# Seven block products for the gate of the last two token groups and the value of groups three and four, with the output projection's products chained in PSUM

## The chip, the cores and the metric

The kernel runs on one core of one Trainium2 chip. The metric is the device time of one execution in microseconds (us); the median of the runs is taken. Matmuls are float16 with float32 sums in PSUM, inputs and output are float32. TensorE is PE (weight loads: PEld), VectorE DVE, ScalarE ACT, GpSimd POOL, SyncE SP.

## The reference

Attention for 4 batches of 8 heads, 768 positions of width 64, then a gated feed-forward layer on all 3072 tokens (512 to 1536 to 512). Heads 0, 2 and 6 see all earlier positions, the others the first 4 and the last 64.

```python
scores = scale * q @ k.T                  # masked: causal, or causal and (first 4 or last 64)
a = softmax(scores)
x = (a @ v), heads side by side           # 3072 x 512
g = x @ w_gate                            # 512 -> 1536
val = x @ w_val
out = (g * sigmoid(g) * val) @ w_out      # 1536 -> 512
```

## The kernel before, in words

**Attention.** The 3072 tokens are 24 tiles of 128. For each tile TensorE makes blocks of scores (L568) in PSUM, ScalarE takes the exponential of up to 1024 columns at a time into a tile `e` (L580), VectorE or GpSimd multiplies the blocks that need it by a mask (L588, 1024 or 640 columns), TensorE multiplies with the values (L598), VectorE divides by the sums (L605, L606), and TensorE turns the result so that tokens lie along columns, tile `xt`. Queries, keys, values and weights come as float32 into staging tiles `raw` by DMA from SP's queue and are cast to float16 on any of the three element-wise engines (L207 on ACT, L209 on POOL, L213 on DVE as a reduction over one element).

**Feed-forward.** Six groups of 512 tokens (g = 0 to 5), twelve hidden slices of 128 (j). A gate or a value of one slice is four matmuls of 512 columns (L760); in the first slices of group 0 it is made in halves. In groups 0 to 3 ScalarE takes a tanh of the gate (L766) and VectorE makes the silu from it (L773); in groups 4 and 5 ScalarE takes silu itself (L782), in place in PSUM. VectorE multiplies silu and value into the hidden tile `h_sb` (L787).

**Seven products.** A product of two matrices cut into 2 x 2 blocks can be made of seven block products instead of eight, with sums of blocks before (left and right) and sums of products after. The output projection is made so in all six groups: sums of blocks of the hidden tile (`hsum`, L844, tiles `h_sb` and `hs_sb`) and of the output weights (`wsum`, L413, tile `wt_sb`), seven products of twelve matmuls of 256 columns (`seventh`, L873), and eight sums or copies of the products into `out_sb` (`gathered`, L899 to L911; a copy is L207 or L209). The value of groups 4 and 5 is made so too: sums of the value weights (`msum`, L1066), of the tokens (`xsum`, L1096), three times seven products of four matmuls of 256 columns per group (`w_product`, L1116; products 6, 7 and 4 are summed onto product 1 in its PSUM room, 3 onto 5), and copies and sums into cells in `raw` tiles (`w_copy`, L207 and L209; `w_add`, L1137). The hidden tile is then made at L1166 from silu in PSUM and the cells.

**PSUM** is one tile `banks` of eight banks. Gate, value, products, scores and attention results each take a bank from it.

**Order.** All work is a list of tasks, one per step and group. Three tables written into the file set everything: ORDER is the order in which the tasks' instructions are issued, WAYS the engine of each task that has a choice (ACT, DVE, POOL or SP), SLOTS the buffer that each task takes from a ring. `Plan.order` reads them and a loop at the end runs the tasks. Each engine has its queue and works it off in that order; a semaphore holds an instruction back until its inputs are made and its buffer is free. ORDER also holds warm-up matmuls on an identity matrix (L322) at the start.

Of the kernel before, what the change touches and what calls it, by code (L numbers as in the profile page):

```python
# [28 lines left out]
    "CN5SCMCR5x5yCOC06O615zCXC17O5eCGC2C36A655kBq0f6v6xBjCYBr725jC47PCIBl718eCHBtBs6Q6U6RBk6VCeBu0eCA"
    "6WCf0c6SCg6B626CCJChCB6TCCBvCiCSBw6DBb70C5Bx6G6eCTByC66yBpC77F6X6Z0d7GBzC86YCZ7HC96a757CCa6n6FCb"  # L30
    "Bm6o817Q6b6c76CqCDCs826dDf7DBnCc77BoDr7E7WCEE1Ds7XDtDcE2Cd7RDu89CrDdE4E3CtDe7U7879DD7A6MCo6gDvDE"
    "7LDgDmDF7BCuE5DGDnCp7VDXCvDHDoDI88DYDZ6z7Y6k7bDJ7S6lDKDS7ZDa6m7j7IDb7JDTDp8f7K7cE6Dq6fDU6p7m6hE7"
    "E8E96i7dDN80EA6jDL6q86Dw7M7a7N6r6sDx7nD06tDODy6u7p7eD1Cw7x7fDM7q8387DP8A7T8D7sCx8BD2Cz7gD3DV7t7o"
    "DhDW7h7rDiD47i7k8EDjEa8ND6D585Cy8G8YD88H7uD7DQ8ZEc7vDR8I8W7y7wEtDk8J8C8X8F8T8QDl8K8L8g8UDzEb8hEu"
    "D98O7l8RE0Ee7z8i8jFNEf8M84Ev8VEgDC8kF0EhDAElEi8SDBEmFf8lEj8PF1EwF8Fg8aEEExEG8bEk8cFiEdF98dEpFjEn"
    "EBF2EqEoFAEyF4FBEDEzECErF3FCEsFQFkFFFRF5FlFGEFFDGQFhEHFmEJFOFPF6GMEKFEFTFSEIF7FWFJGNFXGXFUFYENGR"
    "GOFVFKGSGPFZEOGTFLFHFaGbFMGUFnFrEMFIFoGVHCFpGYFqGfGWGZFbGgFcFsGcGhFdELEPGaGiHDH9EQGdHAGjGeFuGkFe"
    "GqHEGuFtERGvFvGmESHRFwGwHSETGnGoGlEVEWGrEZFzEUHFHBHUHTHGG0GpHXGxHHHIEXHYG2HVH1GsHWHaG1GtHLHZHbHJ"
    "HcGyEYH5H2FxHMGzHOH6G3G5HPH3HdHKG4H0H7G8H4G9H8HeFyHNG7GFG6HQHfHgHlGAGBHhHiHnGDGCGGGIHmGEHjGJGHGK"
    "HzHoHkGLHqHpI3HrHtHvHsHuI4I5HxHwI0I6HyI2I9I7I1ICI8IAIBIDIE"  # L40
# [15 lines left out]
SLOTS = (
    "00142310557834203A728948194837A04374026281030677514571900124020502261616103140412010360010742002"
    "236101614442404106323200562004446120020050132024120000236504202044214005012342616560130400140430"
    "240426501210360012203622541636200122642522142261412021420360620216124236133056022234060254441411"
    "780000311241110210450107121300620173022210651247116100100135016400676677625122602120071100001361"  # L60
    "104112402751261023401751233542301411151104107112101006005400571246015012341114102541540201005110"
    "511141044005511251001120110140204023502454467623349741A203756436562602000262530310914A5433224054"
    "7117736756524224510144"
# [57 lines left out]
def kernel(  # L121
# [13 lines left out]
    nc = tc.nc  # L135
# [87 lines left out]
    SEVENS = 6  # L223
# [530 lines left out]
    hs, gs, sg, sl, vs, o_open, o_sbs = {}, {}, {}, {}, {}, {}, {}  # L754
# [37 lines left out]
    def pieces(g, tt):  # L792


        if g < NG - 1:
            return [("o", 0, DM)]
        if tt < SIZES[g] - 1:
            return [("o", 0, DM)]
        return [("gv", 0, DM - 128), ("gv", DM - 128, DM)]

    def outproj(g, tt, x, js):
        ring, lo, hi = pieces(g, tt)[x]
        if js.start == 0:
            o_open[g, tt, x] = buf(ring, [128, DM], FP, "o_ps")[:, lo:hi]
        for j in range(js.start, js.stop):
            nc.tensor.matmul(
                o_open[g, tt, x], hs[g, j][:, tt * 128:(tt + 1) * 128], wo_sb[:, j, lo:hi],
                start=(j == 0), stop=(j == NJ - 1))

    T_oe, T_st = {}, {}  # L810

    def oevac(g, tt, x):
        if x == 0:
            o_sbs[g, tt] = out_sb[:, tt // 2, tt % 2]
        ring, lo, hi = pieces(g, tt)[x]
        copy(T_oe[g, tt, x], o_sbs[g, tt][:, lo:hi], o_open.pop((g, tt, x)))

    def store(g, tt, x):

        b, i = TILES[FIRST[g] + tt]  # L820
        r0 = b * S + i * 128
        ring, lo, hi = pieces(g, tt)[x]
        eng = nc.scalar if T_st[g, tt, x].way == "ACT" else nc.sync
        eng.dma_start(out=out[r0:r0 + 128, lo:hi], in_=o_sbs[g, tt][:, lo:hi])
# [23 lines left out]
    ONTO = {2: 1, 3: 5}  # L848
    PARTS = [(0, 0, HM), (1, 0, HM)]
    APART = (1, 5)  # L850

    def seventh(g, p, part):
# [9 lines left out]
        on = ONTO.get(p) if g == NG - 1 else None  # L862
# [8 lines left out]
        for x, lo, hi in todo:  # L871
            for j in range(NK):
# [7 lines left out]
    CELLS = {"r1": (1, (1, 0), None), "c11": (2, (0, 0), (1, 0)), "r6": (6, (0, 1), (1, 0)),  # L880
             "r67": (7, (1, 1), (0, 1)), "c21": (4, (1, 0), (1, 1)), "r56": (5, (0, 1), (0, 1)),
             "c22": (5, (1, 1), (1, 1)), "c12": (3, (0, 1), (0, 1))}

# [5 lines left out]
    def gathered(g, name, part):  # L889
        p, to, other = CELLS[name]  # L890
# [22 lines left out]
    def store_cell(g, name, part):  # L913
        x, y = CELLS[name][1]
# [22 lines left out]
    def last_sevens(g, lower, upper, wo, free, old, T_h, product, sums, gather, finish):  # L937
        p1 = product(1, lower + wo, ["big"])
        r1 = gather("r1", [p1], takes=["raw"])
        sums(1, lambda part: [y for j in range(3 * part, 3 * part + 3)  # L940
                              for y in T_h[j] + T_h[j + NK]] + old)
        sums(3, lambda part: [T_hs[g, 1][part]])
        sums(2, lambda part: [T_hs[g, 3][part], p1])
        sums(4, lambda part: [T_hs[g, 2][part]], apart=True)
# [4 lines left out]
        p4 = product(4, upper + T_ws[4], ["o"])  # L949
# [9 lines left out]
        for part in range(2):  # L959
            p2 = product(2, upper + wo + [r1], (), part)  # L960
# [273 lines left out]
    for g in range(NG):  # L1234
# [8 lines left out]
        for j in range(NJ):  # L1243
            parts = [(0, 256), (256, 512)] if g == 0 and j < HALVES else [(0, w)]
            for c in parts:
                below = ("c11", "c21") if j < NK else ("c12", "c22")
                head = "r1" if j < NK else "u2"
                if g in SILU:
                    late = [y for y in P.tasks if y.name.startswith(f"ex{len(TILES) - 1}.")]
                    last_of_g = T_wc["g", g, j % NK // 2, head] if g in WINO["g"] else None  # L1250
                    if last_of_g is None:
# [7 lines left out]
                        if g not in WINO["v"]:  # L1259
                            P.uses(a, "gv", s1)  # L1260
# [118 lines left out]
```

## Time and profile before

| | before |
|---|---|
| median of 3 runs | 237.0 us (236.6 to 237.05) |
| span of the profiled execution | 234.7 us |
| granted TensorE clock | 1.00 |
| busy PE | 229.1 us (98%) |
| busy DVE | 191.6 us (82%) |
| busy ACT | 157.4 us (67%) |
| busy POOL | 137.4 us (59%) |
| DMA, mean | 40.76 MB, 174 GB/s |

The profile is of one execution. A share is busy time over the span. In a slice or a stretch of the span a digit is the busy share in tenths. A row of a timeline has the start and the duration in us, then engine, source line, operation, output and inputs with partitions x columns and type, and in brackets how long the engine was idle before, and what ended that. Two instructions that follow each other on VectorE or GpSimd overlap by up to 0.1 us in the rows.

### The profile page before, as it was taken

To read this page: it belongs to the slowest core of one execution; us is meant where nothing else is said; L and a number is where in the kernel's file an instruction comes from. 1 tells how busy PE (TensorE), PEld (TensorE's weight loads), DVE (VectorE), ACT (ScalarE), POOL (GpSimd) and SP (SyncE) were. 2 spreads that over 40 slices of the span, in tenths; PEclk is the share of its full clock that TensorE was granted. 3 is DMA by queue.
4 is the path that set the end of the run, shared out by engine and by line. 5 is a ranking of instruction groups with operands and counts; after the bars stand their busy time and mean duration, and the time that the engine had idled before them with its cause. 6 is when DMAs were issued, how large, how long until landed. Compare 5 with 4: busy or idle time off the path is not lost.

```text
span 234.7 us, 5842 instructions
## 1 busy us (share of the span) xinstructions
PE 229.1 (98%) x2283; PEld 153.1 (65%) x2283; DVE 191.6 (82%) x347; ACT 157.4 (67%) x254; POOL 137.4 (59%) x151
## 2 busy tenths in 40 slices
PE   7899999999999999999999999999999999999994
PEld 2677865655457778655564556777776767667883
DVE  1889989989999999999879974889968666667864
ACT  3599999679988769856786289767764464463000
POOL 7485499874696300488840887273096960845850
PEclk9999999999999999999999999999999999999999
DMA  6999999999999999998994721700910000220045
GB/s 178 351 343 367 327 336 368 344 341 312 272 258 223 215 246 195 256 169 193 224 235 124 105 45 28 65 3 7 225 39 6 0 0 3 89 89 3 0 183 179
DMA packets 67196, 40.76 MB, mean 174 GB/s; under 512 B 25184, under 2 KB 61024, under 8 KB 67168
## 3 DMA queue, kind: packets, MB, share of 16 engines
q1 hardware_dynamic: 65104, 37.37, 65.0%
q10 hardware_dynamic: 2064, 3.02, 3.7%
q8 instruction: 18, 0.29, 0.5%
q14 instruction: 10, 0.08, 0.1%
HBM read 28.31 MB, written 6.29 MB: 147 GB/s over the span
## 4 chain that ended last, share of the span: by engine, by line
PE 90%; ACT 3%; DMA 2%; SPq 2%; DVE 1%; issue 1%; ACTq 0%
PE banks L760 45%; PE banks L873 24%; PE banks L1116 8%; PE banks L568 6%; PE banks L598 6%; DMA raw<-in_k_dram 2%; ACT e L580 2%; SPq L350 1%; PE banks L474 1%; PE banks L622 1%; DVE xb L606 1%; ACT kT L207 0%; SPq L355 0%; DVE kT L209 0%; ACT hq L207 0%
## 5 line engine op out<-in xcount | busy, mean ns | idle before, releaser
L760 PE MATMUL banks<-xt,wg_sb 128*128 128x512 f16 (+1 forms) x304 | 71.1, 368 | 0.1
L580 ACT ACTIVATE e<-banks 128x1024 f16<-128x1024 f32 (+2 forms) x68 | 59.4, 910 | 10.7 <-PE banks L568 8.5
L760 PE MATMUL banks<-xt,wv_sb 128*128 128x512 f16 (+1 forms) x208 | 48.1, 363 | 0.0
L760 PEld LDWEIGHTS <-wg_sb 128*128 128x128 f16 x304 | 28.6, 98 | 26.1 <-issue 0.5
L873 PEld LDWEIGHTS <-h_sb 128*128 128x128 f16 x420 | 40.2, 98 | 6.9
L766 ACT ACTIVATE sig<-banks 128x512 f32<-128x512 f32 (+1 forms) x52 | 28.8, 567 | 14.6 <-PE banks L760 10.6
L773 DVE SCALAR_TENSOR_TENSOR sil<-sig,banks 128x512 f32<-128x512 f32 (+1 forms) x52 | 32.7, 640 | 4.9 <-ACT sig L766 4.0
L844 POOL TENSOR_TENSOR h_sb<-h_sb 128x768 f16<-128x768 f16 x14 | 22.9, 1639 | 22.7 <-DVE hs_sb L844 17.2
L787 DVE SCALAR_TENSOR_TENSOR h_sb<-sil,banks 128x512 f16<-128x512 f32 (+1 forms) x52 | 32.8, 639 | 2.9 <-PE banks L760 2.6
L588 POOL TENSOR_TENSOR e<-e,m 128x640 f16<-128x640 f16 (+1 forms) x16 | 26.6, 1669 | 7.3 <-ACT e L580 5.6
L911 DVE TENSOR_TENSOR out_sb<-banks,out_sb 128x512 f32<-128x512 f32 x37 | 25.1, 684 | 7.0 <-PE banks L873 6.8
L760 PEld LDWEIGHTS <-wv_sb 128*128 128x128 f16 x208 | 19.1, 98 | 17.4 <-POOL wv_sb L209 0.2
L782 ACT ACTIVATE banks<-banks 128x512 f32<-128x512 f32 x24 | 13.7, 587 | 19.2 <-PE banks L760 19.2
L873 PE MATMUL banks<-wt_sb,h_sb 128*128 128x256 f16 x216 | 26.1, 273 | 0.0
L873 PE MATMUL banks<-wo_sb,h_sb 128*128 128x256 f16 x204 | 25.1, 273 | 0.0
L207 ACT COPY raw<-banks 128x512 f32<-128x512 f32 x26 | 14.8, 593 | 12.0 <-PE banks L1116 6.5
L568 PEld LDWEIGHTS <-kT 64*128 64x128 f16 x472 | 14.5, 94 | 9.4 <-issue 8.9
L209 POOL CAST hq<-raw 128x1024 f16<-128x1024 f32 (+1 forms) x9 | 8.1, 895 | 20.6 <-DMA raw<-in_k_dram 18.8
L568 PE MATMUL banks<-qT,kT 64*128 64x128 f16 x472 | 19.9, 218 | 0.1
L598 PEld LDWEIGHTS <-e 128*128 128x128 f16 x472 | 17.3, 97 | 3.6 <-POOL e L588 0.3
L1166 DVE SCALAR_TENSOR_TENSOR h_sb<-banks,raw 128x512 f16<-128x512 f32 x24 | 15.9, 684 | 4.4 <-ACT banks L782 3.6
L598 PE MATMUL banks<-vt,e 128*128 128x65 f16 x472 | 18.6, 193 | 0.0
(86 smaller groups left out, 320.8 us busy)
## 6 DMA issues: line engine op xcount, KB each, us to landing
raw<-in_v_dram SPq DMA_DIRECT2D x12, 512.0 KB, 6.7
raw<-in_q_dram SPq DMA_DIRECT2D x8, 512.0 KB, 5.7
raw<-in_k_dram SPq DMA_DIRECT2D x8, 512.0 KB, 5.0
raw<-in_moe_w_gate_dram SPq DMA_DIRECT2D x6, 512.0 KB, 8.3
raw<-in_moe_w_val_dram SPq DMA_DIRECT2D x6, 512.0 KB, 8.3
raw<-in_moe_w_out_dram SPq DMA_DIRECT2D x6, 512.0 KB, 8.4
out_dram<-out_sb SPq DMA_DIRECT2D x6, 512.0 KB, 4.0
raw<-in_q_dram SPq DMA_DIRECT2D x8, 256.0 KB, 6.7
```

Source lines behind the costliest of these rows:

```text
L568: nc.tensor.matmul(sc[:, c:c + n, :], weights, moving, start=first, stop=last)
L580: nc.scalar.activation(out=to, in_=src, func=AF.Exp, scale=scale)
L588: ENG[task().way].tensor_tensor(out=ev, in0=ev, in1=mm, op=ALU.mult)
L598: nc.tensor.matmul(avs[t][:, odd, n * 66:n * 66 + 65], ee, vv, start=(m == 0), stop=(m == len(bl) - 1))
L760: nc.tensor.matmul(ps, wsb[:, kk, j * 128:(j + 1) * 128], xt[:, kk, c[0]:c[1]], start=(kk == 0), stop=(kk == 3))
L766: nc.scalar.activation(out=sg[g, j, c], in_=gs[g, j, c], func=AF.Tanh, scale=0.5)
L773: nc.vector.scalar_tensor_tensor(out=sl[g, j, c], in0=sg.pop((g, j, c)), scalar=1.0, op0=ALU.add, in1=gs.pop((g, j, c)), op1=ALU.mult)
L787: nc.vector.scalar_tensor_tensor(out=hs[g, j][:, c[0]:c[1]], in0=sl.pop((g, j, c)), scalar=1.0 if g in SILU else 0.5, op0=ALU.mult, in1=vs ...
L844: ENG[T_hs[g, x][part].way].tensor_tensor(out=to, in0=a, in1=b, op=op)
L873: nc.tensor.matmul(rooms[g, p][:, x, lo:hi], left[:, j, 128 * x:128 * x + 128], right[:, j, lo:hi], start=(on is None and (j == 0 if apart ...
L911: nc.vector.tensor_tensor(out=cell(*to), in0=room, in1=plus, op=ALU.add)
L1116: nc.tensor.matmul(w_rooms[on][:, m], right, left[:, kk], start=(begins and m == 0 and kk == 0), stop=(kk == 1), skip_group_check=True)
```

## The change

- The value of groups 2 and 3, and the gate of groups 4 and 5, are made of seven block products each, like the value of groups 4 and 5 before. So 24 gate tasks and 24 value tasks of four 512-column matmuls go, and 84 block products of four 256-column matmuls come, with their copies and sums, and with sums of the gate weights in the tiles `kT` and `vt` of the attention.
- Where gate and value are both made so (groups 4 and 5), silu is taken cell by cell (`w_silu`, L1134 of the changed kernel) and the hidden tile is made cell by cell: on DVE (L1154) or, new, on POOL (L1151), for 2 slices x 256 tokens.
- In the output projection of groups 0 to 4, products 6, 7 and 4 are summed onto product 1 in its PSUM room, and 3 onto 5 (`CHAIN`). Of the sums, r6, r67 and c21 become copies (u2, u3, c21), and r56 goes. The last group keeps its old form (`CELLS_END`).
- ORDER, WAYS and SLOTS are new. Four warm-up matmuls are fewer.
- Functions that were not in use are removed.

```diff
-    "06000307090A01081U1V0D041cxl1W1X0C021d1f0B20211g1e280g1i2229231h2B2A1j0m1r2C0h1Y1p1s2D1a0F1Z2N1q"
+    "06070A08090D0C0B1U1V031c0200041W011X051d1b1a2022231Y1Z211e0h0n0E0g0m0F0Gy11f1g1h1i1j1p1r2X1q1k1l"
...
-    WINO = {"v": (4, 5), "g": ()}
+    WINO = {"v": (2, 3, 4, 5), "g": (4, 5)}
...
     ONTO = {2: 1, 3: 5}
+    CHAIN = {6: 1, 7: 1, 4: 1, 3: 5}
...
-        on = ONTO.get(p) if g == NG - 1 else None
+        on = (ONTO if g == NG - 1 else CHAIN).get(p)
...
-    CELLS = {"r1": (1, (1, 0), None), "c11": (2, (0, 0), (1, 0)), "r6": (6, (0, 1), (1, 0)),
-             "r67": (7, (1, 1), (0, 1)), "c21": (4, (1, 0), (1, 1)), "r56": (5, (0, 1), (0, 1)),
-             "c22": (5, (1, 1), (1, 1)), "c12": (3, (0, 1), (0, 1))}
+    CELLS = {"r1": (1, (1, 0), None), "c11": (2, (0, 0), (1, 0)), "u2": (6, (0, 1), None),
+             "u3": (7, (1, 1), None), "c21": (4, (1, 0), None),
+             "c22": (5, (1, 1), (1, 1)), "c12": (3, (0, 1), (0, 1))}
...
+    def w_silu(g, s, name):
+        to = w_cell("g", g, s, name)
+        nc.scalar.activation(out=to, in_=w_value("g", g, s, name), func=AF.Silu)
...
+    def w_hidden(g, s, name):
+        j = 2 * s + (0 if name in LOW else NK)
+        x = int(name[1]) - 1
+        to = h_sb[:, g % 2, j:j + 2, 256 * x:256 * x + 256]
+        if T_wh[g, s, name].way == "POOL":
+            nc.gpsimd.tensor_tensor(out=to, in0=w_cell("g", g, s, name),
+                                    in1=w_value("v", g, s, name), op=ALU.mult)
+            return
+        nc.vector.scalar_tensor_tensor(
+            out=to, in0=w_cell("g", g, s, name), scalar=1.0 if g in SILU else 0.5,
+            op0=ALU.mult, in1=w_value("v", g, s, name), op1=ALU.mult)
```

How the new tables move work, at two places. The rows below are the queue's order: line, operation, output and inputs (`x2`: twice in a row). `e` are exponentials and `m` masks, `h_sb` and `hs_sb` the hidden tile and its sums, `wt_sb` sums of output weights `wo_sb`, `wv_sb` value weights, `hq`, `vt` and `kT` cast or turned inputs of the attention, `xt` tokens, `raw` staging tiles and cells, `sig` and `sil` tanh and silu of a gate, `banks` PSUM.

First place: the output projection of the first group. GpSimd's queue before, where the profile has the idle time of 17.74 us between the last two rows:

```order
L413 TENSOR_TENSOR wt_sb<-wo_sb,wt_sb 128x512
L844 TENSOR_TENSOR h_sb<-h_sb 128x3x256
L209 COPY kT_105<-kT_105 128x2x2x2
L209 COPY kT_105<-kT_105 64x2x2
L588 TENSOR_TENSOR e<-e,m_103 128x640
L209 CAST hq<-raw 128x2x8x64
```

GpSimd's queue at the same place in the changed kernel:

```order
L815 TENSOR_TENSOR h_sb<-hs_sb,h_sb 128x3x256
L815 TENSOR_TENSOR h_sb<-h_sb 128x3x256
L416 TENSOR_TENSOR wt_sb<-wo_sb,wt_sb 128x512
L213 CAST hq<-raw 128x2x8x64
L1041 TENSOR_TENSOR raw<-wv_sb,raw 128x768
L416 TENSOR_TENSOR wt_sb<-wo_sb,wt_sb 128x512
L213 COPY kT_104<-kT_104 128x2x2x2
L213 COPY kT_104<-kT_104 64x2x2
L1041 TENSOR_TENSOR raw<-wv_sb 128x768
L213 CAST vt_109<-raw 64x2x2x2x64
L1072 TENSOR_TENSOR raw<-raw,xt 128x512
```

Between the hidden sum and the next cast of queries stood two small copies and one mask; now the sums of output and value weights stand there, on this engine, and the casts of values.

VectorE's queue at this place before:

```order
L844 TENSOR_TENSOR hs_sb<-h_sb 128x768 x2
L844 TENSOR_TENSOR h_sb<-h_sb 128x3x256 x2
L588 TENSOR_TENSOR e<-e,m_101 128x1024
L605 RECIPROCAL rc<-banks 128x8
L606 TENSOR_TENSOR xb<-banks,rc 128x2x4x64
L844 TENSOR_TENSOR h_sb<-hs_sb,h_sb 128x3x256
L588 TENSOR_TENSOR e<-e,m_103 128x640
L588 TENSOR_TENSOR e<-e,m_102 128x1024
L844 TENSOR_TENSOR h_sb<-hs_sb,h_sb 128x3x256
L588 TENSOR_TENSOR e<-e,m_102 128x1024
```

And in the changed kernel:

```order
L776 SCALAR_TENSOR_TENSOR sil<-sig,banks 128x512
L1041 TENSOR_TENSOR raw<-wv_sb 128x768
L416 TENSOR_TENSOR wt_sb<-wo_sb,wt_sb 128x512
L815 TENSOR_TENSOR h_sb<-hs_sb,h_sb 128x3x256
L416 TENSOR_TENSOR wt_sb<-wo_sb 128x512
L591 TENSOR_TENSOR e<-e,m_102 128x1024
L889 TENSOR_TENSOR out_sb<-banks,out_sb 128x2x256
L776 SCALAR_TENSOR_TENSOR sil<-sig,banks 128x512
L815 TENSOR_TENSOR h_sb<-h_sb 128x3x256
L416 TENSOR_TENSOR wt_sb<-wo_sb 128x512
L217 TENSOR_REDUCE vt_109<-raw 64x2x2x2x64
```

Ten operations with both inputs in SBUF (x2 counted twice) came here in two runs, broken by the two of a norm; now seven of them, of four kinds, stand between silu, an output sum and a cast.

Second place: the hidden tile of the last two groups. VectorE's queue before:

```order
L1166 SCALAR_TENSOR_TENSOR h_sb<-banks,raw 128x512 x3
L911 TENSOR_TENSOR out_sb<-banks,out_sb 128x2x256
L1166 SCALAR_TENSOR_TENSOR h_sb<-banks,raw 128x512
L1137 TENSOR_TENSOR raw<-banks,raw 128x512
L1166 SCALAR_TENSOR_TENSOR h_sb<-banks,raw 128x512 x2
L1137 TENSOR_TENSOR raw<-banks,raw 128x512
L844 TENSOR_TENSOR h_sb<-hs_sb,h_sb 128x3x256
L1137 TENSOR_TENSOR raw<-raw 128x512
L1166 SCALAR_TENSOR_TENSOR h_sb<-banks,raw 128x512
```

And in the changed kernel:

```order
L815 TENSOR_TENSOR h_sb<-h_sb 128x3x256
L213 COPY raw<-banks 128x512
L1113 TENSOR_TENSOR raw<-banks,raw 128x512 x6
L1154 SCALAR_TENSOR_TENSOR h_sb<-raw,banks 128x2x256
L1154 SCALAR_TENSOR_TENSOR h_sb<-raw 128x2x256 x2
L815 TENSOR_TENSOR h_sb<-hs_sb,h_sb 128x3x256
L213 COPY raw<-banks 128x512
L1113 TENSOR_TENSOR raw<-raw 128x512
L213 COPY raw<-banks 128x512 x2
L889 TENSOR_TENSOR out_sb<-banks,out_sb 128x2x256
L1113 TENSOR_TENSOR raw<-banks,raw 128x512
```

Multiplications of silu in PSUM with a cell (L1166) alternated with single cell sums; now copies of cells, runs of cell sums and multiplications of two cells (L1154) stand there.

More of the change, by code (lines that the diff above doesn't have):

```diff
@@ L790, in stt2 @@
             in1=vs.pop((g, j, c)), op1=ALU.mult)
[L792 to L824, printed above, removed]
+    T_st = {}
     def blocks(g):
@@ L959, in last_sevens @@
         for part in range(2):
[L960 removed]
+            p2 = product(2, quarter[0, 1] + wo + [r1], (), part)
             c11 = gather("c11", [p2] + free[0], part)
@@ L1077 @@
                     (lambda mat=mat, i=i, kk=kk: msum(mat, i, kk)),
-                    deps=[y for n in range(6) for y in T_w[mat, n]] + before,
-                    takes=(["hq"] if i == 4 else ["e"]) if mat != EARLY
-                    else [] if kk else ["raw"],
+                    deps=[y for n in range(6) for y in T_w[mat, n]] + before
+                    + ([] if mat == EARLY else of_batch(T_sc_of, 2) if i < 3
+                       else of_batch(T_v_of, 2)),
+                    takes=["raw"] if mat == EARLY and kk == 0 else [],
                     after=T_mw[mat, i][:1]))
@@ new lines, with tasks_of_hidden @@
+    T_wh = {}
+    def tasks_of_hidden(g):
+        late = [y for y in P.tasks if y.name.startswith(f"ex{len(TILES) - 1}.")]
+        made = {}
+        for s in range(NK // 2):
+            for name in ("c21", "c11", "c22", "c12"):
+                low, x = name in LOW, int(name[1]) - 1
+                ready = ([T_wp["g", g, s, 4], T_wc["g", g, s, "c11"]] if name == "c21"
+                         else [T_wc["g", g, s, name]])
+                if g in SILU:
+                    s1 = P.add(f"wsl{g}.{s}.{name}", ["ACT"],
+                               (lambda s=s, name=name: w_silu(g, s, name)), deps=ready + late)
+                else:
+                    th = P.add(f"wtn{g}.{s}.{name}", ["ACT"],
+                               (lambda s=s, name=name: w_tanh(g, s, name)), deps=ready,
+                               takes=["sig"])
+                    s1 = P.add(f"wst{g}.{s}.{name}", ["DVE"],
+                               (lambda s=s, name=name: w_stt1(g, s, name)), deps=[th])
+                    P.uses(th, "sig", s1)
+                vready = [T_wp["v", g, s, 4] if name == "c21" else T_wc["v", g, s, name]]
+                was = []
+                if g > 1:
+                    was = [T_p[g - 2, {(1, 0): 6, (1, 1): 7, (0, 0): 3, (0, 1): 4}[low, x]]]
+                    was += T_hs[g - 2, 4] if low and x == 0 else []
+                h = T_wh[g, s, name] = P.add(
+                    f"wh{g}.{s}.{name}",
+                    ["DVE", "POOL"] if g in SILU and name != "c21" else ["DVE"],
+                    (lambda s=s, name=name: w_hidden(g, s, name)), deps=[s1] + vready + was)
+                if name == "c21":
+                    P.uses(T_wp["g", g, s, 1], "gv", s1)
+                    P.uses(T_wp["v", g, s, 1], "gv", h)
+                else:
+                    P.uses(T_wc["v", g, s, "r1" if low else "u2"], "raw", h)
+                P.uses(T_wc["g", g, s, "r1" if low else "u2"], "raw", h)
+                for z in range(2):
+                    made[2 * s + (0 if low else NK) + z, x] = [h]
+        return made
@@ L1242 @@
                 tasks_of_wino(mat, g, xs)
-        for j in range(NJ):
+        if g in WINO["g"]:
+            T_h.update(tasks_of_hidden(g))
+        for j in range(NJ) if g not in WINO["g"] else []:
             parts = [(0, 256), (256, 512)] if g == 0 and j < HALVES else [(0, w)]
@@ L1289 @@
                 was += T_hs[g - 2, 4] if g > 1 and j < NK else []
-                if g not in SILU and g not in WINO["g"]:
+                if g not in SILU:
                     P.uses(th, "sig", s1)
```

259 lines of the change are left out of this document (110 added, 149 removed).

## The prediction

> **What bounds the kernel now.** I read the page's busy times and its 40 slices first.
>
> ```profile
> span 234.7 us, 5842 instructions
> PE 229.1 (98%) x2283; PEld 153.1 (65%) x2283; DVE 191.6 (82%) x347; ACT 157.4 (67%) x254; POOL 137.4 (59%) x151
> PE   7899999999999999999999999999999999999994
> DVE  1889989989999999999879974889968666667864
> POOL 7485499874696300488840887273096960845850
> ```
>
> TensorE has work in 229.1 of 234.7 us, and its slices are full from the third to the last but one. VectorE is second at 191.6 us, and nearly as full in the first half. GpSimd has holes: the 0 3 0 0 and the later 0 are stretches in which it does nothing. The profiled execution has a span of 234.7 us; the median of the runs is 237.0 us, so 2.3 us lie around the span, and I add them to every span below.
>
> Next came the table of stretches (its length, then the busy time and in brackets the instructions of PE, PEld, DVE, ACT and POOL, the granted clock, the DMA share and GB/s), and the chain that ended last, from which I take the price of a matmul.
>
> ```profile
> 0.00:6.00 6.00, 4.64 (x14) 1.69 (x15) 1.05 (x4) 1.90 (x2) 4.66 (x19) 1.00 0.66 181
> 6.00:30.00 24.00, 23.02 (x335) 17.97 (x333) 21.81 (x52) 20.92 (x35) 14.64 (x28) 1.00 1.11 346
> 80.00:93.00 13.00, 13.00 (x188) 10.05 (x186) 12.65 (x25) 10.36 (x16) 0.00 (x0) 1.00 1.20 226
> 180.00:200.00 20.00, 20.00 (x147) 14.10 (x145) 13.73 (x22) 9.46 (x18) 11.44 (x9) 1.00 0.00 1
> 200.00:220.00 20.00, 20.00 (x150) 14.48 (x149) 14.52 (x24) 8.31 (x16) 13.62 (x9) 1.00 0.14 53
> 220.00:234.70 14.70, 11.45 (x105) 10.02 (x103) 8.68 (x16) 0.59 (x1) 5.44 (x4) 1.00 0.41 144
> ```
>
> ```profile
> 57.88 10.36 PE banks L760 x48
> 173.43 2.31 PE banks L1116 x20
> 218.35 13.11 PE banks L873 x120
> ```
>
> TensorE loses 6.00 - 4.64 + 24.00 - 23.02 = 2.3 us at the start, where the loads fill the DMA (shares 0.66 and 1.11), and 14.70 - 11.45 = 3.3 us at the end, where the last results are added and stored. Those 5.6 us are all: in between every us is TensorE's. The granted clock is 1.00 throughout. A matmul of 512 columns takes 10.36/48 = 0.216 us, one of 256 columns 13.11/120 = 0.109 us (0.1155 in the row of the block products at 173.43).
>
> One thing more bears on the change: what VectorE does where GpSimd idles. At 80 to 93 us GpSimd does nothing, and VectorE is busy for 12.65 us. The timeline of GpSimd (start, duration, in brackets the idle time before) and then of both engines, in two places where they work at once:
>
> ```profile
> 97.34 1.04 POOL L209 CAST hq<-raw 128x1024 f16<-128x1024 f32 x1 [17.74 <-DMA raw<-in_k_dram]
> 158.69 1.64 POOL L1066 TENSOR_TENSOR raw<-wv_sb 128x768 f16<-128x768 f16 x1
> 159.76 1.52 DVE L588 TENSOR_TENSOR e<-e,m 128x1024 f16<-128x1024 f16 x2
> 171.36 1.15 POOL L1096 TENSOR_TENSOR raw<-xt,raw 128x512 f16<-128x512 f16 x1
> 172.47 1.72 POOL L1137 TENSOR_TENSOR raw<-raw 128x512 f32<-128x512 f32 x1
> 171.27 0.68 DVE L209 COPY raw<-banks 128x512 f32<-128x512 f32 x1
> 171.87 1.18 DVE L1137 TENSOR_TENSOR raw<-raw 128x512 f32<-128x512 f32 x1
> 172.98 0.68 DVE L1137 TENSOR_TENSOR raw<-banks,raw 128x512 f32<-128x512 f32 x1
> ```
>
> Against these stand the shortest, median and longest duration in ns of the same operations, by source line:
>
> ```profile
> L588 DVE TENSOR_TENSOR e<-e,m x22: 479/680/1121, 23.0 to 167.5; 128x1024 f16<-128x1024 f16 x14, 128x640 f16<-128x640 f16 x8
> L1137 DVE TENSOR_TENSOR raw<-banks,raw x12: 676/686/691, 173.0 to 214.9; 128x512 f32<-128x512 f32 x12
> L1137 DVE TENSOR_TENSOR raw<-raw x2: 685/934/1184, 171.9 to 211.6; 128x512 f32<-128x512 f32 x2
> L1137 POOL TENSOR_TENSOR raw<-raw x4: 1263/1268/1718, 172.5 to 200.4; 128x512 f32<-128x512 f32 x4
> ```
>
> The mask at 159.76 comes 0.57 us before GpSimd's 158.69 row ends (160.33), and takes 1.12 instead of 0.68 us: 0.44 more. The sum at 171.87, both inputs in SBUF, comes 0.64 us before GpSimd's row ends (172.51), and takes 1.18 instead of 0.685 us: 0.50 more. GpSimd's next row then takes 1.72 instead of 1.27: 0.45 more. So each of the two engines waited out the other. The sums with one input in PSUM (banks) keep to 676 to 691 ns, also the one at 172.98, which lies wholly inside GpSimd's 172.47 row. VectorE has 57 operations with both inputs in SBUF (22 masks, 23 hidden sums, 5 sums of value weights, 4 of output weights, 2 cell sums, 1 token sum). These two are the ones that met a running GpSimd operation; the rest stand in its holes.
>
> **The change part by part.** TensorE first. Twenty-four gate tasks and 24 value tasks of four 512-wide matmuls go: 192 x 0.216 = 41.4 us. Eighty-four block products of four 256-wide matmuls come: 336 x 0.109 = 36.7 us (38.8 at 0.1155). Net -4.7 us (-2.6), so 224.4 us of work. Weights for these must be loaded once per matmul, 144 times more; a load takes 98 ns:
>
> ```profile
> L873 PEld LDWEIGHTS <-h_sb 128*128 128x128 f16 x420 | 40.2, 98 | 6.9
> ```
>
> It hides under a 109 ns matmul, with 11 ns to spare; without that cover 336 loads would add 33 us, but the existing block products run at 109 with the same loads. Four warm-up matmuls go too, at nothing, since loads bound that stretch. Chaining products 6, 7 and 4 onto 1, and 3 onto 5, changes no matmul. Of twenty additions on VectorE it turns fifteen into copies (eleven on ScalarE, four on VectorE) and takes out five, the sums r56.
>
> The element-wise engines, by groups of one shape (columns: busy us, mean ns of one, idle before):
>
> ```profile
> L209 POOL CAST vt<-raw 64x512 f16<-64x512 f32 x18 | 10.9, 607 | 2.1 <-DMA raw<-in_v_dram 1.3
> L209 POOL CAST hq<-raw 128x1024 f16<-128x1024 f32 x6 | 6.2, 1037 | 18.7 <-DMA raw<-in_k_dram 18.2 <-DVE m L287 0.3 <-DMA kT<-hq 0.2
> L209 POOL COPY vt<-vt 2x330 f16<-2x330 f16 x14 | 6.3, 452 | 6.2 <-PE banks L598 5.9
> L209 POOL COPY kT<-kT 128x8 f16<-128x8 f16 x6 | 1.1, 190 | 2.0 <-PE banks L568 1.8
> L588 POOL TENSOR_TENSOR e<-e,m 128x640 f16<-128x640 f16 x10 | 13.9, 1396 | 5.8 <-ACT e L580 4.3 <-issue 1.5
> L588 POOL TENSOR_TENSOR e<-e,m 128x1024 f16<-128x1024 f16 x6 | 12.7, 2123 | 1.4 <-ACT e L580 1.4
> L1066 POOL TENSOR_TENSOR raw<-wv_sb 128x768 f16<-128x768 f16 x3 | 4.9, 1642 | 0.0
> L1096 POOL TENSOR_TENSOR raw<-xt 128x512 f16<-128x512 f16 x4 | 4.6, 1159 | 0.1
> L213 DVE TENSOR_REDUCE hq<-raw 128x1024 f16<-128x1024 f32 x4 | 4.8, 1210 | 0.0
> ```
>
> GpSimd, from the counts of its queue: casts of 1024 columns 15 to 28 (+13 x 1.04 = 13.5), of 512 columns 25 to 32 (+7 x 0.61 = 4.3), the small copies +14 (eight at 0.45, six at 0.19: 4.7), weight sums 3 to 8 (+5 x 1.64 = 8.2), token sums 7 to 11 (+4 x 1.16 = 4.6), cell sums 4 to 13 and the nine new products of gate and value (+18 x 1.27 = 22.9; the products are not in the trace, and the float32 sum of the same size is the nearest row), one hidden sum more and one output-weight sum less (+0.5), and masks 10 and 6 to 8 and 4 (-2 x 1.40 - 2 x 2.12 = -7.0). Together +51.7 us: 137.4 becomes 189 us.
>
> VectorE starts operations of 512 columns 0.60 us apart when it does not wait (171.27 to 171.87 above). By the counts of its queue it gets 27 more cell sums, 20 more cell copies, 4 output copies and 15 products of gate and value, and loses 24 multiplications and 20 output sums: 22 more, 13.2 us. Seven casts at 1.21 us move away, -8.5 us, and the small rest (masks +4, sums of weights and tokens +8, short casts and evictions fewer) adds about 3, an estimate from rows of 0.42 to 0.69 us. So 191.6 becomes 199.3 us. ScalarE gets 39 copies and loses casts: about 163 us, no bound.
>
> By work alone TensorE would stay the bound. But VectorE's operations with both inputs in SBUF grow from 57 to 80 (26 masks, 22 hidden sums, 8 weight sums, 5 token sums, 5 output-weight sums, 5 cell sums, 9 products), and the queues as listed put them beside GpSimd's new work, not in holes: at the first group's output projection, where GpSimd sat idle for 17.74 us, it now has a dozen operations in a row. With 189 us of work in a span of 232 to 247 us GpSimd runs 0.77 to 0.81 of the time; I take 0.8, so 80 x 0.8 = 64 of them meet it. Each costs VectorE 0.44 to 0.50 us, 0.47 in the mean of the two rows. The bounds are 0 (they fall into what holes remain) and a whole GpSimd operation, 1.0 to 1.6 us; I take the measured value. 64 x 0.47 = 30 us, and VectorE is busy for 199.3 + 30 = 229 us, more than TensorE's 224.4.
>
> [...]
>
> **How the sum comes out.** VectorE cannot be busy all the time. In the trace it idles 6.00 - 1.05 = 4.95 us at the start and 14.70 - 8.68 = 6.0 us at the end, and these stay. From 180 to 220 us it idles 6.3 + 5.5 = 11.8 us waiting for TensorE; there the new kernel has more for it (cells of gate and value of the last group), so I keep a third, 4 us. 229 + 4.95 + 6.0 + 4 = 244.3 us of span, with 2.3 around it 246.6: I say 247. TensorE then has 244.3 - 224.4 = 20 us of waits, of which 5.6 are those of now.
>
> **The rivals.** [...]
>
> [...]
>
> *Full blocking* (slower still): a GpSimd operation of 1.16 to 1.64 us met at a random instant has 0.7 us left, and successive operations of VectorE each wait for one. 64 x 0.7 = 45 us instead of 30, the rest as above: 262. For it: the 0.45 us that GpSimd lost at 172.47. Against: the smaller two prices.
>
> **How the numbers follow.** Forecast (VectorE bound by the ports) 0.74; ports cheap 0.13; gain eaten 0.05; full blocking 0.08. The predicted time is the forecast's, 247. The range reaches down to 235, into the cheap case, and up to 257, which is 0.6 us a meeting with half the idle time of 180 to 220 kept (199.3 + 38.4 + 11 + 6 + 2.3); it leaves out the full blocking, about half of the cheap case and a little of the forecast's upper end, some 0.17. A measurement of this kernel can tell about 0.2%, 0.5 us. Faster by more has the cheap case and a part of the eaten gain, 0.14; within it 0.03; slower 0.83.
>
> **What would show it.** Right: masks, sums and products of VectorE with both inputs in SBUF with a median well above 0.68 and 0.55 us, longest over 1.5; VectorE over 95% busy from 30 to 200 us; GpSimd 80% or more; gates and block products on TensorE waiting for VectorE, some 20 us in all; TensorE's own busy time near 224 us. [...]

## The result and the profile after

The changed kernel takes 266.7 us (median of 4 runs, 265.0 to 268.6), the kernel before 236.8 us on the same chip: ratio 1.127, 95% interval 1.121 to 1.132. Slower was forecast, at 247 us and at most 257; it is 30 us slower and outside the range. The profiled execution, the longest of the four, has a span of 266.8 us. (Times of runs below leave out executions over 1.5% longer than the run's fastest, one of them at a TensorE clock of 0.75, and no row shown is from one; two expected texts quote 247 and 245.6 us, medians with them.)

The page of the changed kernel, busy times and slices:

```profile
span 266.8 us, 6230 instructions
PE 236.6 (89%) x2423; PEld 169.9 (64%) x2423; DVE 232.7 (87%) x373; ACT 165.2 (62%) x266; POOL 202.5 (76%) x208
PE   7889989799959869969989998976999899999884
DVE  2888969869998985999999999998889789999993
POOL 7489899939965955699909999977975796898710
PEclk9999999799989989999999999999799999999999
```

TensorE, full before from the third slice on, now has holes everywhere. VectorE went from 191.6 to 232.7 us, but stands at 87%: neither engine is busy all the time. GpSimd's empty stretches of before are gone. And TensorE's clock, 1.00 throughout before, falls to 0.7 and 0.8 in four slices.

The stretches (length, then busy us of PE, PEld, DVE, ACT, POOL with instructions, clock, DMA share, GB/s):

```profile
30.00:60.00 30.00, 26.65 (x292) 15.14 (x289) 24.24 (x46) 22.11 (x34) 24.65 (x29) 0.94 1.19 307
60.00:90.00 30.00, 26.27 (x228) 14.17 (x225) 27.86 (x40) 18.75 (x27) 24.22 (x26) 0.94 0.95 206
120.00:150.00 30.00, 28.68 (x291) 19.30 (x290) 29.13 (x47) 20.91 (x36) 21.72 (x23) 1.00 0.60 142
150.00:180.00 30.00, 26.87 (x270) 18.46 (x268) 29.21 (x45) 19.70 (x32) 27.63 (x23) 1.00 0.53 97
```

From 120 to 180 us VectorE is the bound, at 97%. From 30 to 60 us it is busy for only 24.2 of 30 us, and TensorE for 26.7. The longest waits between 30 and 60 us (who waited for whom: us in total, times, longest) show a round of three:

```profile
DVE sil L776 <- ACT sig L769: 4.2, 3, 2.4
ACT sig L769 <- PE banks L763: 3.5, 4, 1.6
PE banks L763 <- ACT e L583: 1.8, 1, 1.8
PE banks L477 <- ACT e L583: 1.5, 1, 1.5
```

VectorE waits for a tanh of ScalarE, ScalarE's tanh for a gate of TensorE, and TensorE for exponentials of ScalarE.

VectorE's operations by line (shortest, median, longest in ns): masks, three groups of hidden sums, and cell sums with one input in PSUM and with none:

```profile
L591 DVE TENSOR_TENSOR e<-e,m x26: 479/1028/2120, 22.3 to 198.1; 128x1024 f16<-128x1024 f16 x16, 128x640 f16<-128x640 f16 x10
L815 DVE TENSOR_TENSOR h_sb<-h_sb x8: 541/1158/1714, 61.4 to 254.1; 128x768 f16<-128x768 f16 x8
L815 DVE TENSOR_TENSOR h_sb<-hs_sb,h_sb x7: 544/558/1619, 86.1 to 255.9; 128x768 f16<-128x768 f16 x7
L815 DVE TENSOR_TENSOR hs_sb<-h_sb x5: 543/551/2042, 60.4 to 251.6; 128x768 f16<-128x768 f16 x5
L1113 DVE TENSOR_TENSOR raw<-banks,raw x36: 673/681/692, 114.5 to 256.9; 128x512 f32<-128x512 f32 x36
L1113 DVE TENSOR_TENSOR raw<-raw x5: 692/1342/1679, 111.5 to 239.6; 128x512 f32<-128x512 f32 x5
```

The masks' median went from 680 to 1028 ns, the longest from 1121 to 2120. The cell sums with a PSUM input keep to 673 to 692 ns, 36 times out of 36. That is the mark of the meetings: of these rows only those with both inputs in SBUF have longer operations. Not all of them do: in two of the three groups of hidden sums the median stays at 0.55 us. Taking for each of the 80 such operations the shortest duration of its shape in the traces off its own, 44 are longer by over 0.1 us, by 36 us together: 0.82 us each.

One place shows how it comes to 0.82 instead of 0.47. The timeline of VectorE, GpSimd and TensorE (start, duration):

```profile
69.91 1.20 DVE L416 TENSOR_TENSOR wt_sb<-wo_sb 128x512 f16<-128x512 f16 x1
71.04 1.39 DVE L1041 TENSOR_TENSOR raw<-wv_sb 128x768 f16<-128x768 f16 x1
72.46 1.88 DVE L1041 TENSOR_TENSOR raw<-wv_sb,raw 128x768 f16<-128x768 f16 x1
74.26 1.63 DVE L591 TENSOR_TENSOR e<-e,m 128x1024 f16<-128x1024 f16 x1
75.82 0.67 DVE L790 SCALAR_TENSOR_TENSOR h_sb<-sil,banks 128x512 f16<-128x512 f32 x1
70.78 1.23 POOL L213 CAST hq<-raw 128x1024 f16<-128x1024 f32 x1
71.97 1.95 POOL L815 TENSOR_TENSOR hs_sb<-h_sb 128x768 f16<-128x768 f16 x1
73.89 1.46 POOL L416 TENSOR_TENSOR wt_sb<-wo_sb 128x512 f16<-128x512 f16 x1
75.43 1.49 POOL L416 TENSOR_TENSOR wt_sb<-wo_sb,wt_sb 128x512 f16<-128x512 f16 x1
76.55 1.02 PE L763 MATMUL banks<-xt,wg_sb 128*128 128x512 f16 x4 [2.89 <-DVE h_sb L790]
```

Four two-input operations of VectorE stand in a row beside a full GpSimd queue. They are longer than the shortest of their kind by 0.79, 0.84, 1.33 and 0.95 us: each by the time that GpSimd's running operation had left when it began (0.93 us for the first, beside a sum of output weights from 69.68 to 70.84), all but 0.13 to 0.14 us. GpSimd's next operations are longer too (1.95, 1.46 and 1.49 us instead of 1.64 and 1.16). The four take 6.1 us, where by the shortest rows (0.41, 0.55, 0.55, 0.68) they would take 2.2. Behind them stands the multiplication of 75.82, which frees the bank that a gate on TensorE waits for: 2.89 us.

The waits also cost clock. TensorE's clock (the third number from the end) after a wait of 1.84 us that ends at 49.7 us:

```profile
48.00:50.00 2.00, 0.27 (x2) 0.15 (x2) 1.83 (x6) 2.00 (x3) 1.86 (x3) 1.00 1.02 333
50.00:52.00 2.00, 2.00 (x7) 0.78 (x6) 1.78 (x2) 0.66 (x2) 1.94 (x2) 0.54 1.11 346
52.00:54.00 2.00, 2.00 (x10) 0.95 (x8) 1.24 (x2) 0.58 (x1) 1.92 (x3) 0.60 1.06 388
```

Seven matmuls in 2 us, then ten (14 and 20 at full clock, in the run below): for about 3.4 us the granted clock is half. The mean clock is 0.974, which is 6.9 us of the span; in the other three executions it is 0.981 to 0.987, or 5.1 to 3.4 us. Of this the prediction had nothing, since the clock of before is 1.00 everywhere.

### The profile page after: what moved, and what is told of

Its sections match the earlier page's. It is cut to its first block, busy times and chain, and to the rows that moved or that the text cites. A ratio compares the mean times of both kernels' runs of the same rounds, so it can differ in the third digit from the quotient of the medians.

```text
span 266.8 us, 6230 instructions
## 1 busy us (share of the span) xinstructions
PE 236.6 (89%) x2423; PEld 169.9 (64%) x2423; DVE 232.7 (87%) x373; ACT 165.2 (62%) x266; POOL 202.5 (76%) x208
## 3 DMA queue, kind: packets, MB, share of 16 engines
q10 hardware_dynamic: 1520, 1.97, 2.1%
## 4 chain that ended last, share of the span: by engine, by line
DVE 53%; PE 24%; issue 9%; DMA 7%; ACT 5%; POOL 1%; SPq 1%; DVEq 0%; ACTq 0%; POOLq 0%
PE banks L763 7%; PE banks L1092 7%; DVE e L591 6%; PE banks L845 6%; DVE raw L1113 6%; DVE h_sb L1123 5%; DVE banks L776 4%; DVE h_sb L790 3%; DVE h_sb L815 3%; DMA raw<-in_moe_w_gate_dram 3%; DVE h_sb L1154 3%; DVE xb L609 3%; DVE raw L213 3%; DVE sil L776 3%; DVE out_sb L889 2%
## 5 line engine op out<-in xcount | busy, mean ns | idle before, releaser
L763 PE MATMUL banks<-xt,wg_sb 128*128 128x512 f16 (+1 forms) x208 | 49.9, 370 | 6.2 <-DVE h_sb L790 2.9
L211 ACT COPY raw<-banks 128x512 f32<-128x512 f32 x54 | 29.7, 589 | 24.3 <-PE banks L1092 17.7
L591 DVE TENSOR_TENSOR e<-e,m 128x1024 f16<-128x1024 f16 (+1 forms) x26 | 28.5, 1103 | 0.1
L763 PE MATMUL banks<-xt,wv_sb 128*128 128x512 f16 (+1 forms) x112 | 27.2, 376 | 0.0
L1113 DVE TENSOR_TENSOR raw<-banks,raw 128x512 f32<-128x512 f32 x36 | 23.4, 681 | 3.1 <-ACT raw L211 2.5
L213 POOL CAST vt<-raw 64x512 f16<-64x512 f32 x29 | 20.2, 698 | 4.3 <-DMA raw<-in_v_dram 3.1
L1113 POOL TENSOR_TENSOR raw<-raw 128x512 f32<-128x512 f32 x13 | 17.7, 1359 | 5.7 <-DVE raw L213 4.4
L776 DVE SCALAR_TENSOR_TENSOR sil<-sig,banks 128x512 f32<-128x512 f32 (+1 forms) x28 | 16.7, 604 | 5.7 <-ACT sig L769 5.3
L790 DVE SCALAR_TENSOR_TENSOR h_sb<-sil,banks 128x512 f16<-128x512 f32 (+1 forms) x28 | 16.5, 605 | 5.5 <-PE banks L1092 2.9
L1092 PEld LDWEIGHTS <-raw 128*128 128x128 f16 x192 | 18.4, 98 | 4.2 <-issue 1.4
```

Of the source, the lines that this page charges most:

```text
L211: nc.scalar.copy(out=dst, in_=src)
L591: ENG[task().way].tensor_tensor(out=ev, in0=ev, in1=mm, op=ALU.mult)
L763: nc.tensor.matmul(ps, wsb[:, kk, j * 128:(j + 1) * 128], xt[:, kk, c[0]:c[1]], start=(kk == 0), stop=(kk == 3))
L776: nc.vector.scalar_tensor_tensor(out=sl[g, j, c], in0=sg.pop((g, j, c)), scalar=1.0, op0=ALU.add, in1=gs.pop((g, j, c)), op1=ALU.mult)
L1092: nc.tensor.matmul(w_rooms[on][:, m], right, left[:, kk], start=(begins and m == 0 and kk == 0), stop=(kk == 1), skip_group_check=True)
L1113: ENG[T_wc[mat, g, s, name].way].tensor_tensor(out=to, in0=other, in1=to, op=ALU.add)
```

## The experiments

Two theories, named as the expected texts name them: the ports theory (VectorE's operations with two SBUF inputs and GpSimd's operations with SBUF inputs lengthen each other where they meet; the name is the author's, and no run shows what the two engines share), and the order theory (the new sequence makes TensorE wait for copies, exponentials and PSUM rooms whatever the meetings do).

**Meetings put into the old kernel.** GpSimd gets work that nobody needs, in its empty stretches, once reading SBUF, once only writing.

```diff
+    def extra(n):
+        for _ in range(n):
+            nc.gpsimd.tensor_tensor(out=scratch, in0=ident.unsqueeze(1).to_broadcast([128, 4, 128]),
+                                    in1=ident.unsqueeze(1).to_broadcast([128, 4, 128]), op=ALU.add)
...
             P.tasks[number].run()
+            extra({"mask10.1": 12, "vw3.1v": 6}.get(P.tasks[number].name, 0))
```

> The kernel before, with 18 extra GpSimd additions of 512 columns (1.16 us each, inputs in SBUF, result used by nobody) in two stretches where GpSimd has nothing to do (12 at 79.6 us, 6 at 160.3 us), beside 14 and 10 two-input operations of VectorE. Ports theory: 20 or so meetings at 0.75 us, 15 us on VectorE, of which the first stretch, where VectorE is 97% busy, gives 6 to 9 us to the end: 242 to 248 us. Order theory: GpSimd's extra work is in nobody's way, 236.5 to 237.5 us.

> As the run with extra additions, but each addition replaced by two memsets of 512 columns (0.52 us each by the rows of shorter ones), which read nothing from SBUF. Ports theory with the read side as what is shared: VectorE's sums and masks keep their length, 236.5 to 238 us. If any work of GpSimd blocks them: as the run with additions, 242 to 248 us. Order theory: 236.5 to 237.5 us.

Measured: with the additions 245.0 us, ratio 1.035 (1.033 to 1.037); with two memsets for each addition 236.6 us, ratio 1.000 (0.999 to 1.001). The masks of VectorE, and the extra instructions, of the run with additions:

```profile
L595 DVE TENSOR_TENSOR e<-e,m x22: 483/684/1523, 23.1 to 175.6; 128x1024 f16<-128x1024 f16 x14, 128x640 f16<-128x640 f16 x8
L209 POOL TENSOR_TENSOR scratch<-ident x18: 1039/1232/1487, 79.6 to 172.0; 128x512 f16<-128x512 f16 x18
```

And of the run with memsets (the second of each pair stands on the next line of the code, with 18 more):

```profile
L595 DVE TENSOR_TENSOR e<-e,m x22: 477/682/1119, 23.1 to 167.6; 128x1024 f16<-128x1024 f16 x14, 128x640 f16<-128x640 f16 x8
L209 POOL MEMSET scratch<- x18: 524/524/539, 79.7 to 166.2; 128x512 f16 x18
```

Eighteen additions that nobody waits for cost 8.2 us; nearly as long spent on writing (36 x 0.524 = 18.9 us, against 21.5) costs nothing, and the longest mask stays at 1119 ns, a meeting that was there before. With the additions, 16 of VectorE's 57 two-input operations are longer by over 0.1 us, by 9.9 us together (2 by 0.9 us before): fewer and cheaper meetings than the 15 us that were expected. With the memsets, 21 others ran beside a memset, and none is longer by more than 0.02 us (the hidden sums keep to 543 to 558 ns; with the additions the longest takes 1390). Here the ports theory is right, and of these two kinds of GpSimd work only the one that reads SBUF counts: 8.2 us against none.

**Meetings taken out of the changed kernel.** Each of the 80 operations becomes a reduction of one SBUF input that takes about as long (masks and hidden sums on every second column).

```diff
+    def lone(dst, src):
+        nc.vector.tensor_reduce(out=dst, in_=src.unsqueeze(len(src.shape)),
+                                axis=mybir.AxisListType.X, op=ALU.max)
...
+        if task().way == "DVE":
+            ev = es[t, u][:, at:at + (8 if m is m1 else m.shape[1]), 0:128:2]
+            lone(ev, ev)
+            return
```

> The changed kernel with VectorE's 80 operations of two SBUF inputs made into reductions of one SBUF input that take about as long (half the columns for masks and hidden sums; sums of weights and tokens full length, 0.3 to 0.4 us longer each, some 5 us in all): masking, the second addend and the second factor are left out there. Order, engines, buffers and GpSimd's work stay. Ports theory: VectorE's 36.5 us of lengthening go, GpSimd's 15 us too; TensorE is the bound again, 234 to 242 us. Rival, the order itself (waits on ScalarE's copies, PSUM rooms held longer): 258 to 267 us, TensorE still waits 20 us or more.

> The changed kernel with only VectorE's 26 masks made into reductions of one SBUF input and the same time (no masking on VectorE). They hold 13.1 of the 36.5 us of lengthening. Ports theory: 8 to 15 us come back, 252 to 259 us. Order theory: within 2 us of the changed kernel, 264 to 268 us.

Measured: without any meetings 247.2 us (ratio 1.041, 1.034 to 1.048), between the two expected ranges; with only the masks freed 259.1 us (1.097, 1.092 to 1.102), at the edge of what the ports theory said, where 25 us of lengthening are left of 36. Neither theory is whole: the meetings hold 19 to 20 of the 30 us, with all that follows from them, and 10 us stay without them.

**The same with zero tokens,** a control for the values that the leaving out makes.

```diff
-        nc.vector.reciprocal(out=rc, in_=av[:, :, :, 64:65])
+        nc.vector.tensor_scalar(out=rc, in0=av[:, :, :, 64:65], scalar1=0.0, op0=ALU.mult,
+                                scalar2=0.0, op1=ALU.add)
```

> The kernel before, with the reciprocal of the softmax sums replaced by a multiplication with zero, so that all tokens of the feed-forward layer, and all that is made of them, are zero (same instructions, same sizes). A control for data: if the clock and the time do not hang on the values, 236 to 237.5 us at clock 1.00.

> The changed kernel with all tokens zero in the same way. If the dips of the granted clock (four of some 3.4 us at half rate) come from TensorE's own idle times, they stay: 264 to 268 us, clock about 0.975. If they come from what the data draw, they go: 258 to 261 us at clock 1.00. Ports theory: VectorE's lengthening stays 36 us either way.

> The changed kernel without VectorE's two-input operations (one-input reductions as before; masking, second addends and second factors left out) and with all tokens zero, since the run with the values that this gave had a TensorE clock of 0.75 in its profile. Ports theory: 234 to 241 us at clock 0.99 or more, TensorE idle for less than 5 us in the middle. Order theory: 250 us or more at that clock.

Measured: 236.6, 266.8 and 246.3 us (ratios 1.000, 1.129 and 1.040). The tokens' values make no difference, and the half clock stays with zeros (0.981 in the changed kernel): it does not come from these values. The third run says it again: without meetings 246 to 247, not 235. The page and the longest waits of TensorE (us in total, times, longest), of the same kernel with two moves in TensorE's queue that are described below:

```profile
PE 228.8 (93%) x2423; PEld 167.8 (68%) x2423; DVE 203.9 (83%) x373; ACT 165.2 (67%) x266; POOL 187.6 (77%) x208
PE banks L488 <- ACT e L594: 1.5, 1, 1.5
PE banks L1118 <- ACT raw L219: 1.5, 2, 0.9
PE banks L616 <- DVE out_sb L909: 1.2, 1, 1.2
```

The longest waits behind the start now name ScalarE: exponentials, and copies of the new products' cells. Over the whole trace TensorE waits 4.0 us for VectorE, where it was 18.7 in the changed kernel and 0.8 before.

**Casts given to ScalarE,** a complete kernel with less of GpSimd.

```diff
             t.way = t.ways[int(w)]
+            if t.way == "POOL" and "ACT" in t.ways and t.name[:2] in ("cx", "sv", "sk"):
+                t.way = "ACT"
```

> The changed kernel, complete, with GpSimd's 49 small casts and copies of the attention's keys, values and queries given to ScalarE (some 26 us), at the same places in the order. Ports theory: GpSimd runs 0.65 instead of 0.76 of the time, about 10 of the 49 meetings go: 5 to 10 us less, 256 to 262 us, unless ScalarE's queue now holds up exponentials. Order theory: no gain, 265 us or more.

Measured: 281.7 us, ratio 1.190 (1.184 to 1.196), 15 us more than the changed kernel. The order theory had 265 us or more; the ports theory's gain did not come, but what it named as its exception did. The meetings fell (30 us of lengthening instead of 36), but what stands behind the casts in ScalarE's queue now comes late: exponentials are waited for 21.4 us by GpSimd's masks, copies of keys 5.8 us by TensorE. Two rows of the run's waits:

```profile
POOL e L593 <- ACT e L585: 21.4, 5, 7.9
PEld L573 <- ACT kT L213: 5.8, 4, 3.9
```

**TensorE's waits filled, and two of them shortened.** First, 37 matmuls on the identity in the longest waits; second, two moves in its queue; then both (29 matmuls).

```diff
+        named = {t.name: k for k, t in enumerate(self.tasks)}
+        for name, n, at in (("gate0.7.0", 8, 4), ("gate1.10.0", 12, 2), ("sc13.0", 7, 6),
+                            ("sc22.0", 5, 3), ("val21.1", 5, 3)):
+            numbers.insert(numbers.index(named[name]), self.FILL + n + 16 * at)
...
+        for name, other, after in (("vals0.11.0", "gate0.7.0", 0), ("trk4", "gate0.10.0", 1)):
+            numbers.remove(named[name])
+            numbers.insert(numbers.index(named[other]) + after, named[name])
```

> The changed kernel, complete, with 37 extra matmuls of 512 columns on the identity (result unused) put into TensorE's longest waits: 8 at 47.9 us, 12 at 73.7, 7 at 94.3, 5 and 5 at 183 to 185, each into a PSUM bank that is free there. If the four stretches at half clock (3.4 us each, 1.7 us lost in each) follow from idle time, they go, and 2 to 7 us come back: 260 to 265 us at clock 0.99 or more. If they do not, or if VectorE sets the pace so that TensorE's speed does not count: 266 to 268 us.

> The changed kernel, complete, with the same two moves in TensorE's queue. Order theory: the two waits (1.5 and 1.8 us) and one stretch at half clock (1.7 us) shrink by 3 to 4 us: 262.5 to 264 us. Ports theory: VectorE sets the pace behind them, less than 1.5 us comes back: 265 to 267 us.

> The changed kernel, complete, with both the extra matmuls in the waits (29, without the 8 at 47.9 us) and the two moves in TensorE's queue. If both savings add: 261 to 263 us. If VectorE's meetings are all that counts behind them: 264 to 266 us.

Measured: filled 263.8 us (ratio 1.114, 1.113 to 1.116), moved 264.9 us (1.119, 1.115 to 1.123), both 263.6 us (1.114, 1.112 to 1.116). The place of before, now with the extra matmuls:

```profile
48.00:50.00 2.00, 1.91 (x9) 0.87 (x9) 1.83 (x6) 1.94 (x3) 1.88 (x2) 1.00 1.01 338
50.00:52.00 2.00, 2.00 (x14) 1.03 (x13) 2.00 (x2) 0.64 (x2) 1.94 (x2) 1.00 1.10 324
52.00:54.00 2.00, 2.00 (x20) 0.99 (x20) 1.93 (x4) 1.14 (x2) 1.92 (x3) 1.00 1.06 395
```

The half clock is gone here, and 2.9 us of the whole with it: useless work made the kernel faster. So the half clock here follows from the wait. In the mean of four executions each, half clock takes 4.7 us of the changed kernel and 0.8 us of this run; of the 3.9 us between them 2.9 come back. The profiled execution still has one stretch at half clock, a new one, after a wait of 2.05 us at 117 us: its clock is 0.991, that of the other three 0.999. The moves alone cannot be told from no gain: their interval overlaps that of the changed kernel (1.121 to 1.132).

**What is left without meetings.** The run without meetings and with zero tokens gets the two moves, then light work on VectorE (masks and most hidden sums cut to a sixteenth of their columns, not the eighth that is named below), then on ScalarE (exponentials and tanh on a quarter of their columns or less; `e` and `sig` are constant tiles filled at the start).

```diff
+            ev = es[t, u][:, at:at + (8 if m is m1 else m.shape[1]), 0:128:16]
...
+            to, src = to[:, :, 0:32], src[:, :, 0:32]
         nc.scalar.activation(out=to, in_=src, func=AF.Exp, scale=scale)
```

> The run without meetings (one-input reductions on VectorE, tokens zero, 247 us) with two moves in TensorE's queue: the value of slice 11 of group 0 ahead of the gate of slice 7, which waits 1.9 us for two exponentials, and the turning of the keys of pair 4 behind the gate of slice 10, where it waits 1.5 us. Theory that the 10 us left without meetings are the order's own waits: 242 to 245 us. If they are VectorE's load: 246 to 248 us.

> As the run with two moves, and VectorE's masks and hidden sums cut to an eighth of their columns (some 17 us of VectorE's work left out). TensorE alone: 224.4 us of work, 5.6 at the ends and 2.3 around the span, 232.3 us. If VectorE's load is what holds the run without meetings above that: 233 to 238 us. If it is the order's waits on ScalarE and PSUM rooms: 241 us or more.

> As the run with light VectorE work and no meetings (245.6 us), and ScalarE's exponentials and tanh cut to a quarter or less of their columns (tiles set to a constant at the start; about 60 us of ScalarE's work left out; its copies of cells stay). If the 10 us that the change costs without meetings are waits for ScalarE's exponentials and tanh, TensorE alone is left: 233 to 237 us. If they are PSUM rooms held by the new products until their copies and sums are done, or the DMA: 242 us or more.

Measured: 245.7, 244.7 and 242.2 us (ratios 1.037, 1.036 and 1.023). The two moves bring nothing clear of noise here either (1.040 before them). VectorE's load, without the meetings, holds nothing up: 10 us less of its work changed the ratio by 0.001. So it does not matter either that the reductions take 7 us more in all than the 196.7 us of VectorE's work without meetings. ScalarE's long operations hold about 3 us, the difference of the last two ratios. That run's start lost some more to the filling of the tiles (a new wait of 2.64 us at 6.4 us, then 3.4 us at half clock: 0.93 in the mean from 6 to 30 us), so the true share may be larger, by some 4 us at most (2.64 and half of 3.4). With 242.2 us the run lies at the expected edge of PSUM rooms or DMA, and far from TensorE alone. The page of the run with light VectorE work, a stretch, a wait, and a run of block products:

```profile
PE 226.3 (93%) x2423; PEld 166.9 (69%) x2423; DVE 193.6 (80%) x373; ACT 165.1 (68%) x266; POOL 187.5 (77%) x208
90.00:120.00 30.00, 26.32 (x258) 19.12 (x257) 22.61 (x43) 19.56 (x32) 23.24 (x22) 1.00 0.82 153
PE banks L1118 <- ACT raw L219: 2.3, 2, 1.6
206.51 7.00 PE banks L1118 x64
```

TensorE's work is 226.3 us at clock 1.00, and a block product's matmul takes 7.00/64 = 0.109 us. But from 90 to 120 us, where the value of the third group is made of block products for the first time, TensorE loses 3.7 us, and 2.3 of these are the waits for copies of cells in the third row.

## Why the prediction was right and wrong

**TensorE's work: right.** 224.4 us were worked out; 226.3 are measured at full clock, in the run with light VectorE work, against 229.1 before. (The 236.6 us of the changed kernel hold the half clock.) The matmul's 0.109 us held. The gain of 2.8 us is real, and is lost many times over.

**The other engines' work: right.** VectorE 199.3 worked out; 232.7 less 36 is 196.7. GpSimd 189; 187.6 in the run without meetings and with two moves. (One reading of the page is off: the slices that the prediction quotes as 0 3 0 0 are 3 0 0, and single zeros follow. Nothing was worked out from them.)

**The meetings: there as predicted, both factors off.** 64 at 0.47 us were taken, 30 us in all; 44 at 0.82 us came, 36 us. The price was read from two lone meetings. In the new queues two-input operations stand in runs beside GpSimd operations in runs, and each waits for most of one (0.8 to 1.3 us in the four rows above). The rival of full blocking had 0.7 us a meeting and 262 us, with a chance of 0.08; its price and its time were nearer than the forecast's. VectorE's busy time came out at 232.7 where 229 were forecast, so this term is 4 us of the miss.

**VectorE's idle time: this step failed.** "VectorE cannot be busy all the time": 15 us of idling were kept, 34.1 us are there (266.8 less 232.7). The span is 22.5 us longer than the 244.3 us of the sum: 19 are this term, 6 the meetings, and VectorE's work is 2.6 less. The step let go the 20 us that VectorE idled from 6 to 180 us before (43.1 in all, less 5.0, 6.0 and 11.8), as if an engine near its limit were always fed. The forecast of over 95% busy from 30 to 200 us holds only from 120 to 180. Instead of one bound engine there are several that wait in turn. Over the whole trace TensorE waits 18.7 us for VectorE, about the 20 us that were forecast, and VectorE in turn waits 12.4 us for TensorE and 10.3 for ScalarE. VectorE's idle time elsewhere did not absorb such delays here: in the run with the additions 9 us of new lengthening cost 8.2 us, in a kernel where VectorE idled for 43 us. That the order must put the slack where the delay is, is how we read this; no run changed the order of VectorE's and GpSimd's work to show it.

**TensorE's waits without meetings: too small.** The lower end of the range, 235 us, is the case of cheap meetings: 232.3 us (224.4 + 5.6 + 2.3) and 2.7 us for more waits of TensorE. These 2.7 us were the author's estimate, and no run shows them. With the meetings removed the kernel takes 245 to 247. So of the 30 us about 20 are the meetings (266.7 to 247) and 10 are the order's own (236.8 to 247): 2.8 us less work, and some 13 us more of waits and half clock. Shown of these are only ScalarE's exponentials and tanh, with about 3 us. Of the rest the profile of the run with light VectorE work shows waits where the third group's block products begin (3.7 us lost from 90 to 120 us) and 1.5 us more lost than before in the first 30 us, but no run took these apart: none changed the PSUM rooms or the copies of cells alone, since the tables that fix rooms and order hold for one list of tasks only. That stays open.

**The clock: not seen.** All sums took 1.00. The profile of before has no wait of TensorE as long as a microsecond once it has started (the longest is 0.8 us), so it could not show what one costs. In the changed kernel half clock takes 3.4 to 6.9 us (clock 0.987 to 0.974). Where a wait was filled it went (1.00 instead of 0.54 and 0.60 from 50 to 54 us); it is part of both shares above.

## What to carry to other kernels

Before moving work to GpSimd, count VectorE's operations with both inputs in SBUF that will run beside its reads, and price each at most of a GpSimd operation when either side stands in a run (0.82 us in the mean of 44 here); a PSUM input on VectorE (36 of 36 sums at 673 to 692 ns), or a memset on GpSimd (ratio 1.000), cost nothing here. An order that keeps the two apart was worth some 20 us here, more than the 3 us of matmuls saved, and looked only like idle time on GpSimd. When the sum over one engine nears the sum over another, do not take the larger for the span: here both waited.

## What the runs showed of the hardware that was not expected

In the changed kernel's trace the clock falls to half four times, each time for 3.41 us, from 50.17, 77.47, 97.95 and 186.70 us on: after waits of TensorE of 1.84, 2.89 and 1.68 us, and after two of 1.2 us within 3 us. Waits of 1.50 us at 33.0 and 1.60 us at 116.8 us were not followed by it. With the masks freed, waits of 1.92 and 1.97 us were not (clock 1.00 from 46 to 58 and from 70 to 82 us), and one of 1.68 us was (0.80 and 0.77 from 90 to 98 us), so the length of a wait alone did not decide here. Eight matmuls on the identity in the wait of 1.84 us kept the clock at 1.00 from 48 to 54 us.

In the 3.41 us just before each of the four stretches TensorE idled for 1.86, 2.49, 1.83 and 2.43 us. It idled for 1.84 us from 115.02 to 118.43 us too, and there the clock stayed at 1.00 in the 3.41 us that follow. What makes the difference is not shown by these runs.
